# Sliding-window attention and a squared-ReLU FFN on one core: one planned order for all engines, over pairs of chunks

## The chip, the cores and the metric

The kernel runs on one core of one Trainium2 chip. The metric is the device time of one execution in microseconds (us). The engines are TensorE (PE, with its weight loads as PEld), VectorE (DVE), ScalarE (ACT), GpSimd (POOL) and SyncE (SP). Each engine takes its instructions in the order in which the program lists them. All DMAs here are issued from SP's queue.

## What is computed

Heads of 64 columns, a causal window of 64 keys, then a feed-forward layer over the heads put side by side:

```python
def _attn_ref(q, k, v):                    # (8, 8, 576, 64): batch, heads, tokens, columns
    scores = scale * np.matmul(q, k.transpose(0, 1, 3, 2))
    mask = (rel >= 0) & (rel < window)     # rel: query minus key; window = 64
    attn = softmax(np.where(mask, scores, -1e9))
    return np.matmul(attn, v)

def _moe_ref(x, w_in, w_out):              # x: (4608, 512), w_in: (512, 2048), w_out: (2048, 512)
    h = np.maximum(x @ w_in, 0.0)
    return h * h @ w_out
```

Inputs and output are float32; the kernel multiplies in fp16.

## The kernel before

The 4608 tokens (the batches one after the other) are 36 chunks of 128. A chunk's k, q and v are fetched as float32 (`fetch`, L100 to L110; one DMA of 256 KB each in runs of 256 bytes, two where a batch ends inside the chunk) and cast to fp16 by POOL (L200, L204, L208). POOL also moves the values by 64 partitions (`shift_v`, L212 and L214), since each block of 64 queries needs the 128 keys that end with it, and these must begin at partition 0. k and q are turned so that the head columns lie on partitions: the first 14 chunks by PE (`T`, L252) and copies out of PSUM (L267, L273), the others by a DMA transpose of 512 columns each (L276, L279). For the keys of the pair before, DVE copies 64 columns (`halo`, L240).

Attention of one chunk: scores (`S_`, L290, 16 matmuls of 64 columns), exp on ACT (L297), the mask as a minimum on DVE (L303), probabilities times values (`V`, L315), reciprocal and normalising on DVE (L322, L323). The result x is turned by PE (`X`, L334, first 16 chunks) or by a DMA transpose (`dma_xT`, L342).

The up-product (x times w_in) has two forms. For the first eight chunks `U` (L364) makes four blocks of 128 x 128 in one PSUM bank. For the groups of 512 tokens after that `UP` (L387) makes one block of 128 x 512 with four matmuls. ACT takes the ReLU out of PSUM (L371, L391); the square is ReLU times the PSUM value on DVE (L375, L395) or a Square on ACT (L381, L393); its place is the tile h2, of which there are two (512 tokens each).

The down-product of group 0 is plain (`O`, L431, 512 columns). From group 1 on it uses seven products of half size in place of eight (`out_seven`, L442): DVE forms sums of blocks of h2 (`hsum`, L456), PE multiplies them with prepared sums of w_out (`product`, L464, 256 columns), and ACT or DVE takes the banks out with the additions (`evac`, L478, L480). The sums of w_out are made once on DVE (`w_out_sum`, L412 to L418). w_in is scaled on DVE (L217), w_out cast on POOL (L222).

[...]

The order of work is set in two ways. Up to the first rounds it is the word list `FIRST`, which is issued word by word for all engines and for SP's queue: `fk0` fetches k of chunk 0, `fw0` a quarter of w_in, `T0` transposes, `U2.1` an up-product, `r` and `s` ReLU and square, `o` casts of w_out, `ws` its sums. It fetches chunks 0 to 3, then the four quarters of w_in (1 MB each), then the rest; w_out comes after chunk 7. From group 2 on, a loop gives each piece a fraction of the round and sorts by it:

```python
        ev = even(out_seven(g - 1))
        if g < NTB:
            ev += [(0.05 + 0.95 * t, s) for t, s in even([lambda f=f: UP(g, f) for f in range(FFC)])]
        if g + 1 < NTB:
            ev += attention(g + 1)
            ev += loads(4 * g + 6)
        for _, s in sorted(ev, key=lambda e: e[0]):
```

So in round g the down-product of group g-1 is interleaved with the up-product of group g, and between them stands the attention of group g+1, whose x goes to a DMA transpose at fractions 0.275 and 0.735 of the round.

Of the kernel before, what the change touches and what calls it, by code (L numbers as in the profile page):

```python
# [15 lines left out]
SQ_ACT = (0, 2, 4, 6, 8, 10, 12, 14)  # L16
FIRST = '''
fk0 fq0 fv0 fk1 fq1 kc0 fv1 qc0 T0 W4 fk2 vc0 ck0 cq0 vd0 fq2 S0 W6 ea0 fv2 kc1 eb0 ma0 qc1 fk3
mb0 vc1 T1 fq3 kc2 V0 W5 ck1 cq1 vd1 n0 fv3 S1 ea1 X0 fw0 qc2 eb1 ma1 x0 vc2 T2 mb1 vd2 ck2 cq2 V1
fw1 n1 S2 e2 kc3 fw2 X1 qc3 fw3 x1 fk4 m2 vc3 T3 fq4 vd3 ck3 cq3 V2 n2 S3 e3 X2 x2 m3 V3 n3 w0.0  # L20
X3 w0.1 x3 w0.2 w0.3 U0.0 U1.0 r0.0 fv4 w1.0 sa0.0 w1.1 U2.0 w1.2 r1.0 w1.3 U3.0 s1.0 r2.0 s2.0
U0.1 r3.0 w2.0 sa3.0 w2.1 U1.1 r0.1 w2.2 w2.3 U2.1 s0.1 r1.1 s1.1 U0.2 r2.1 fk5 w3.0 w3.1 U1.2
r0.2 w3.2 w3.3 sa0.2 U2.2 s2.1 fq5 kc4 r1.2 U0.3 s1.2 r2.2 fv5 qc4 s2.2 U1.3 r0.3 fk6 vc4 s0.3 T4
vd4 r1.3 fq6 U2.3 ck4 cq4 sa1.3 fv6 kc5 S4 r2.3 U3.1 qc5 fk7 e4 s2.3 vc5 T5 fq7 kc6 U3.2 r3.1 m4
cq5 vd5 ck5 V4 sa3.1 S5 n4 r3.2 fv7 U3.3 qc6 e5 fo0 vc6 X4 sa3.2 x4 T6 vd6 m5 r3.3 U4.0 fo1 ck6
cq6 s3.3 fo2 V5 kc7 r4.0 fo3 S6 n5 qc7 U4.1 e6 fk8 vc7 s4.0 fq8 X5 vd7 r4.1 U4.2 m6 x5 s4.1 V6
r4.2 T7 n6 U5.0 cq7 ck7 s4.2 X6 r5.0 o0 S7 x6 U4.3 e7 o1 s5.0 o2 U5.1 r4.3 m7 o3 s4.3 U5.2 r5.1
s5.1 V7 r5.2 fv8 o4 U6.0 n7 o5 s5.2 U5.3 o6 r6.0 o7 s6.0 X7 r5.3 U6.1 x7 o8 s5.3 U6.2 o9 r6.1
sa6.1 o10 ws0.0 U7.0 r6.2 ws1.0 o11 sa6.2 U6.3 ws0.1 r7.0 ws1.1 U7.1 r6.3 s7.0 fk9 o12 sa6.3 U7.2
o13 r7.1 fq9 kc8 ws0.2 U7.3 r7.2 s7.1 o14 fv9 sa7.2 O0.0 ws1.2 qc8 r7.3 fk10 ws2.0 vc8 T8 ws2.1  # L30
s7.3 O1.0 o15 fq10 cq8 ck8 vd8 O2.0 fv10 ws0.3 ws1.3 S8 ws2.2 kc9 O3.0 ws2.3 e8 qc9 fk11 vc9 O0.1
m8 fq11 vd9 T9 V8 ck9 cq9 fv11 O1.1 kc10 n8 fk12 qc10 S9 vc10 X8 e9 O2.1 fq12 x8 kc11 O3.1 vd10 m9
fv12 fk13 V9 qc11 T10 n9 O0.2 vc11 fq13 cq10 ck10 kc12 X9 S10 vd11 x9 O1.2 e10 fv13 T11 qc12 m10
fk14 O2.2 vc12 cq11 ck11 fq14 kc13 V10 S11 vd12 n10 fv14 O3.2 e11 X10 fk15 qc13 O0.3 m11 vc13 x10
fq15 V11 kc14 oe0 st0 T12 n11 vd13 fv15 O1.3 cq12 ck12 X11 qc14 oe1 st1 T13 x11 O2.3 vc14 ck13
cq13 vd14 O3.3 oe2 st2 oe3 st3 kc15 qc15 vc15 vd15
'''
# [3 lines left out]
def kernel(  # L41
# [15 lines left out]
    NCK = NT // P  # L57
    NB = S // 64
# [5 lines left out]
    NTB = NT // 512  # L64
    FQ = DFF // 4
    KH = FFC // 2
    NH = DM // 2
    NFIRST = 8

    const = ctx.enter_context(tc.tile_pool(name="const", bufs=1))  # L70
    stage = ctx.enter_context(tc.tile_pool(name="stage", bufs=17))
    st16 = ctx.enter_context(tc.tile_pool(name="st16", bufs=8))
    attw = ctx.enter_context(tc.tile_pool(name="attw", bufs=3))
    smallp = ctx.enter_context(tc.tile_pool(name="smallp", bufs=4))
    xtp = ctx.enter_context(tc.tile_pool(name="xtp", bufs=3))
    h2pool = ctx.enter_context(tc.tile_pool(name="h2pool", bufs=2))
    hrp = ctx.enter_context(tc.tile_pool(name="hrp", bufs=3))
    ps_up = ctx.enter_context(tc.tile_pool(name="ps_up", bufs=2, space=bass.MemoryType.PSUM))
    ps_out = ctx.enter_context(tc.tile_pool(name="ps_out", bufs=2, space=bass.MemoryType.PSUM))
    ps_att = ctx.enter_context(tc.tile_pool(name="ps_att", bufs=2, space=bass.MemoryType.PSUM))  # L80

    ctx.enter_context(tc.manual_schedule())


    put_off = []

    def later(n, fn):
        put_off.append([n, fn])

    def tick():  # L90
        for e in list(put_off):
            e[0] -= 1
            if e[0] <= 0:
                put_off.remove(e)
                e[1]()


    sts, k16s, q16s = {}, {}, {}

    def fetch(nm, i):  # L100
        src = {"k": k, "q": q, "v": v}[nm]
        b0, j0 = divmod(2 * i, NB)
        st = stage.tile([P, H, D], FP32, name=f"{nm}_st", tag="st")
        if j0 + 1 < NB:
            nc.sync.dma_start(
                out=st[:], in_=src[b0, :, 64 * j0:64 * j0 + P, :].rearrange("h p d -> p h d"))
        else:
            nc.sync.dma_start(
                out=st[0:64], in_=src[b0, :, 64 * j0:S, :].rearrange("h p d -> p h d"))
            nc.sync.dma_start(  # L110
                out=st[64:P], in_=src[b0 + 1, :, 0:64, :].rearrange("h p d -> p h d"))
        sts[nm, i] = st

    w_in_sb = const.tile([P, DMC, DFF], FP16, name="w_in_sb")
    w_out_sb = const.tile([P, FFC, DM], FP16, name="w_out_sb")
    wb_all = const.tile([P, 3, KH, NH], FP16, name="wb_all")
    hs_all = const.tile([P, 2, KH, 256], FP16, name="hs_all")
    early = h2pool.tile([P, FFC, 512], FP16, name="early", tag="h2")  # L120
    wb = [wb_all[:, i] for i in range(3)]

    def as_stage(ap, c=4):
        return ap.bitcast(FP32).rearrange("p (c n) -> p c n", c=c)


    tick_of = smallp.tile([P, 16], FP32, name="tick", tag="tick", bufs=1)
    nc.vector.memset(tick_of[:, 0:1], 0.0)
    nc.scalar.activation(out=tick_of[:, 1:2], in_=tick_of[:, 0:1], func=AF.Exp)

    def await_load(nm, i):

        nc.scalar.activation(out=tick_of[:, 1:2], in_=sts[nm, i][:, 0, 0:1], func=AF.Copy)

    wb_stage = as_stage(wb_all[:, 0:2].rearrange("p i k n -> p (i k n)"))
    hs_stage = as_stage(hs_all[:].rearrange("p i k n -> p (i k n)"))
    w_in_stage = [as_stage(early[:, 0:8].rearrange("p f t -> p (f t)")),
                  as_stage(early[:, 8:16].rearrange("p f t -> p (f t)")),
                  wb_stage, hs_stage]
    osb_all = const.tile([P, 3, 2, DM], FP32, name="osb_all")  # L140
    w_out_stage = [wb_stage, hs_stage, osb_all[:, 0:2].rearrange("p i m d -> p (i m) d"),
                   (as_stage(wb_all[:, 2].rearrange("p k n -> p (k n)"), 2), osb_all[:, 2])]

    def w_out_staged(f):
        at = w_out_stage[f // 4]
        return at[f % 4 // 2][:, f % 2] if f // 4 == 3 else at[:, f % 4]

    def fetch_w_in(quar):
        nc.sync.dma_start(
            out=w_in_stage[quar],  # L150
            in_=moe_w_in[:, quar * FQ:(quar + 1) * FQ].rearrange("(c p) n -> p c n", p=P))

    def fetch_w_out(quar):
        at = w_out_stage[quar]
        for n, part in enumerate(at if quar == 3 else (at,)):
            rows = 512 if quar < 3 else 256
            r0 = quar * 512 + n * rows
# [49 lines left out]
    def cast_v(i):  # L207
        nc.gpsimd.tensor_copy(out=v_evs[i % NV][:, :, 0:D], in_=sts["v", i][:])  # L208

# [429 lines left out]
```

## Time and profile before

| What | Value |
|---|---|
| Median of three timed runs | 314.78 us (313.43 to 315.09) |
| Span of the profiled execution, first to last instruction | 312.6 us |
| Mean TensorE clock granted in it | 0.973 of full speed |
| First up-product starts | 24.3 us |
| First round of seven products starts | 87.7 us |
| DMA: packets, bytes, share of 16 engines | 157,077; 55.05 MB; 75.8% on the main queue |

The page gives no other time of the profiled execution than its span. "Busy" counts the time in which an engine has an instruction under way; for PE that includes matmuls at a lower clock, so a busy PE isn't one at its best. The lines by stage have the busy time of each engine in a stretch of the span, with the granted clock (1.00 is full speed) and the DMA engines' share beside it. A line by instruction has minimum, median and maximum duration in ns.

### The profile page before, as it was taken

To read this page: it belongs to the slowest core of one execution; us is meant where nothing else is said; L and a number is where in the kernel's file an instruction comes from. 1 tells how busy PE (TensorE), PEld (TensorE's weight loads), DVE (VectorE), ACT (ScalarE), POOL (GpSimd) and SP (SyncE) were. 2 spreads that over 40 slices of the span, in tenths; PEclk is the share of its full clock that TensorE was granted. 3 is DMA by queue.
4 is the path that set the end of the run, shared out by engine and by line. 5 is a ranking of instruction groups with operands and counts; after the bars stand their busy time and mean duration, and the time that the engine had idled before them with its cause. 6 is when DMAs were issued, how large, how long until landed. Compare 5 with 4: busy or idle time off the path is not lost.

```text
span 312.6 us, 8069 instructions
## 1 busy us (share of the span) xinstructions
PE 289.9 (93%) x3263; PEld 201.3 (64%) x3263; DVE 215.4 (69%) x398; ACT 178.3 (57%) x282; POOL 134.6 (43%) x203
## 2 busy tenths in 40 slices
PE   3858899998998989999999999999996999999995
PEld 1448888965565656666666666666663666666684
DVE  4665959997676766875878486758766567546392
ACT  1333697762575647584766577576654575566500
POOL 4930888989833534371637353543254300000000
PEclk9955999999999999999999999999999899999999
DMA  7998999999669629899997799898799920400123
GB/s 181 230 363 243 228 271 388 210 219 221 151 186 211 132 66 242 178 153 138 274 171 166 185 238 166 169 221 203 151 154 210 220 59 19 151 2 0 69 102 102
DMA packets 157077, 55.05 MB, mean 176 GB/s; under 512 B 147824, under 2 KB 148848, under 8 KB 157040
## 3 DMA queue, kind: packets, MB, share of 16 engines
q1 hardware_dynamic: 157040, 54.54, 75.8%
q8 instruction: 25, 0.41, 0.6%
q14 instruction: 12, 0.10, 0.1%
HBM read 36.70 MB, written 9.44 MB: 148 GB/s over the span
## 4 chain that ended last, share of the span: by engine, by line
PE 77%; DVE 10%; ACT 7%; DMA 2%; issue 2%; SPq 0%; ACTq 0%
PE hps L387 30%; PE opsC L464 9%; PE opsD L464 8%; PE opsA L464 8%; PE hps L364 5%; PE opsB L464 4%; PE av L315 4%; PE sc L290 3%; PE ops L431 3%; ACT pm L297 2%; PE warm L403 2%; ACT hrelu L371 2%; DVE x_sb L323 2%; DVE pm L303 2%; DVE w_in_sb L217 1%
## 5 line engine op out<-in xcount | busy, mean ns | idle before, releaser
L387 PE MATMUL hps<-xT,w_in_sb 128*128 128x512 f16 x448 | 113.7, 382 | 3.0 <-DMA xT<-x_sb 2.7
L391 ACT ACTIVATE hrelu<-hps 128x512 f32<-128x512 f32 x112 | 66.8, 598 | 76.0 <-PE hps L387 75.9
L464 PEld LDWEIGHTS <-h 128*128 128x128 f16 x640 | 62.4, 98 | 23.0 <-issue 2.5
L387 PEld LDWEIGHTS <-w_in_sb 128*128 128x128 f16 x448 | 42.5, 98 | 36.2 <-DMA xT<-x_sb 2.9
L395 DVE SCALAR_TENSOR_TENSOR h<-hps,hrelu 128x512 f16<-128x512 f32 x56 | 38.6, 690 | 36.9 <-ACT hrelu L391 36.5
L200 POOL CAST k<-k_st 128x512 f16<-128x512 f32 x36 | 25.2, 701 | 79.6 <-DMA k_st<-in_k_dram 79.2
L297 ACT ACTIVATE pm<-sc 128x1024 f16<-128x1024 f32 (+1 forms) x38 | 35.6, 977 | 12.3 <-PE sc L290 12.3
L393 ACT ACTIVATE h<-hrelu 128x512 f16<-128x512 f32 x56 | 35.3, 630 | 1.8
L364 PE MATMUL hps<-xT,w_in_sb 128*128 128x128 f16 x512 | 33.6, 227 | 1.9 <-DVE h L375 1.3
L208 POOL CAST v_ev<-v_st 128x512 f16<-128x512 f32 x36 | 25.7, 713 | 18.8 <-DMA v_st<-in_v_dram 17.8
L364 PEld LDWEIGHTS <-w_in_sb 128*128 128x128 f16 x512 | 31.2, 102 | 2.9 <-issue 1.4
L464 PE MATMUL opsD<-wb_all,h 128*128 128x256 f16 x256 | 32.9, 273 | 0.0
L464 PE MATMUL opsA<-w_out_sb,h 128*128 128x256 f16 x240 | 31.9, 278 | 0.5
L464 PEld LDWEIGHTS <-hs_all 128*128 128x128 f16 x256 | 25.1, 98 | 8.9
L303 DVE TENSOR_TENSOR pm<-pm,mask_inner 128x1024 f16<-128x1024 f16 (+1 forms) x29 | 22.3, 769 | 9.5 <-ACT pm L297 9.4
L204 POOL CAST q<-q_st 128x512 f16<-128x512 f32 x35 | 24.0, 684 | 7.1 <-DMA q_st<-in_q_dram 6.5
L371 ACT ACTIVATE hrelu<-hps 128x512 f32<-128x512 f32 x32 | 18.8, 595 | 13.4 <-PE hps L364 12.1
L212 POOL COPY v_od<-v_ev 64x512 f16<-64x512 f16 x36 | 25.0, 696 | 2.3
L323 DVE TENSOR_TENSOR x_sb<-av,rden 128x512 f16<-128x512 f32 x36 | 24.9, 691 | 1.2
L214 POOL COPY v_od<-v_ev 64x512 f16<-64x512 f16 x35 | 24.9, 711 | 2.0
L480 DVE SCALAR_TENSOR_TENSOR osb_all<-opsD,u 128x512 f32<-128x512 f32 x16 | 11.0, 690 | 12.0 <-PE opsD L464 12.0
L375 DVE SCALAR_TENSOR_TENSOR h<-hps,hrelu 128x512 f16<-128x512 f32 x22 | 14.7, 681 | 6.3 <-ACT hrelu L371 6.2
(71 smaller groups left out, 331.1 us busy)
## 6 DMA issues: line engine op xcount, KB each, us to landing
k_st<-in_k_dram SPq DMA_DIRECT2D x32, 256.0 KB, 3.8
q_st<-in_q_dram SPq DMA_DIRECT2D x32, 256.0 KB, 4.2
v_st<-in_v_dram SPq DMA_DIRECT2D x32, 256.0 KB, 4.3
out_dram<-osb_all SPq DMA_DIRECT2D x14, 512.0 KB, 3.6
early<-in_moe_w_in_dram SPq DMA_DIRECT2D x2, 1024.0 KB, 8.8
out_dram<-osb_all SPq DMA_DIRECT2D x8, 256.0 KB, 2.2
wb_all<-in_moe_w_in_dram SPq DMA_DIRECT2D x1, 1024.0 KB, 11.4
hs_all<-in_moe_w_in_dram SPq DMA_DIRECT2D x1, 1024.0 KB, 15.4
```

Of the source, the lines that this page charges most:

```text
L200: nc.gpsimd.tensor_copy(out=k16s[i][:], in_=sts["k", i][:].rearrange("p h d -> p (h d)"))
L208: nc.gpsimd.tensor_copy(out=v_evs[i % NV][:, :, 0:D], in_=sts["v", i][:])
L297: nc.scalar.activation(out=pms[i][:, part], in_=scs[i][:, part], func=AF.Exp, scale=1.0 / float(D) ** 0.5)
L303: nc.vector.tensor_tensor(out=pms[i][:, part], in0=pms[i][:, part], in1=mask[:].rearrange("p (o a) r -> p o (a r)", o=1) .to_broadcast([P, ...
L323: nc.vector.tensor_tensor(out=xs[i][:], in0=avs[i][:, :, :, 0:D], in1=rden[:].to_broadcast([P, 2, 4, D]), op=ALU.mult)
L364: nc.tensor.matmul(hps[:, f, :], w_in_sb[:, c, (4 * fq + f) * P:(4 * fq + f + 1) * P], xT_of(g)[:, c, t0:t0 + P], start=(c == 0), stop=(c ...
L371: nc.scalar.activation(out=hr_of[i, fq][:], in_=hps_of[i, fq][:], func=AF.Relu)
L387: nc.tensor.matmul(hps[:], w_in_sb[:, c, f * P:(f + 1) * P], xT_of(g)[:, c, :], start=(c == 0), stop=(c == DMC - 1))
L391: nc.scalar.activation(out=hrelu[:], in_=hps[:], func=AF.Relu)
L393: nc.scalar.activation(out=h2_of(g)[:, f, :], in_=hrelu[:], func=AF.Square)
L395: nc.vector.scalar_tensor_tensor(out=h2_of(g)[:, f, :], in0=hps[:], scalar=0.0, in1=hrelu[:], op0=ALU.max, op1=ALU.mult)
L464: nc.tensor.matmul(banks[bank][:, m, :], a[:, kk, m * P:(m + 1) * P], w[:, kk], start=(first and kk == 0 and m == 0), stop=(kk == KH - 1), ...
```

## The change

Everything between setup and launch is written anew around a planner. Each operation is named and given a key (its priority), the engines that may run it with an assumed duration in us for each, the operations it comes after, and the buffers it uses. `Plan.order` then walks through time and issues operations one after the other; that sets the order on each engine and on SP.

```diff
+            for o in live:
+                t = opens(o)
...
+                ready = max(o["ready"], t)
...
+                w = min(((max(engines[r[0]], ready) + r[1], r[1], n)
+                         for n, r in enumerate(o["runs"])))
+                r = o["runs"][w[2]]
+                start = max(engines[r[0]], ready)
+                late = max(start - engines[r[0]], 0.0)
+                rank = (round(late, 1), o["key"])
```

`opens` gives the time at which the buffers are free. For each engine the operation with the shortest wait (in tenths of a us), and among these the lowest key, is next; where several engines may run it, the one that would be done first. A handoff to another engine counts 0.15 us, a DMA's landing 2.2 us after its end.

The buffers, all with fixed sizes:

```diff
+    plan.pool("wst", wb + hs)
+    plan.pool("st", tiles("st", NSTAGE, [P, 1024], FP32))
+    plan.pool("kq16", tiles("kq16", 4, [P, 1024], FP16))
+    plan.pool("kT", tiles("kT", 4, [P, HP, PT], FP16))
...
+    plan.pool("xT", tiles("xT", 5, [P, 2, DMC, P], FP16))
+    plan.pool("h2", tiles("h2", 4, [P, FFC, PT], FP16))
+    plan.pool("f2k", tiles("f2k", 12, [P, 512], FP32))
...
+    plan.pool("att", tiles("att", 2, [P, 2, 512], FP32, psum))
+    plan.pool("bk", tiles("bk", 4, [P, 512], FP32, psum))
```

`NSTAGE` is 6 (two pairs' k, q and v; before, 17 tiles of half the size). `h2` holds 256 tokens a tile. The four banks `bk` serve up-products, down-products and transposes alike; `att` serves scores and PV. `f2k` holds ReLU outputs, partial sums and output tiles.

The unit is a pair of chunks (256 tokens, 18 pairs). k and v are fetched in two DMAs a pair as before; q in one, two tokens to a partition, so a run is 512 bytes; the score block then has its columns in the order r, i, and is written to PSUM with a step of two:

```diff
+    def fetch_q(name, p):
...
+                in_=q[b, :, s:s + m, :].rearrange("h (p r) d -> p h (r d)", r=2))
...
+        scv = sc[:].rearrange("p a (h b i r) -> p a h b r i", h=HP, b=2, r=2)
...
+                    if n == 0:
+                        prev = at(f"kT.{p - 1}")[rs, hp, 192:256] if p else kT[rs, hp, 0:64]
+                        nc.tensor.matmul(scv[0:64, hh, hp, blk], prev, mv, start=True, stop=True)
+                        nc.tensor.matmul(scv[64:P, hh, hp, blk], kT[rs, hp, 0:64], mv,
+                                         start=True, stop=True)
```

The `halo` copy is gone: the first block of a pair reads the pair before. k, q and x of pairs 0 to 7 are turned by PE (eight transposes into one bank, one copy out by DVE or ACT), of pairs 8 to 17 by one DMA transpose of 1024 columns each. The order of the loads on SP is by keys (lowest first):

```diff
+    LOAD_KEYS = {0: -100, 1: -94, 2: -88, 3: -82, 4: -76, 5: -70}
+    WIN_KEYS = [-99, -98, -93, -92, -91, -90, -87, -86]
+    WOUT_KEYS = [-81, -80, -79, -78, -75, -74, -73, -72]
...
+        return LOAD_KEYS.get(p, p / 2 - 3.0)
```

So two eighths of w_in (512 KB each) come after pair 0, four after pair 1, two after pair 2; four eighths of w_out after pair 3, four after pair 4. Casts of k and q of pairs 0 to 3 and of the weights may run on POOL, DVE or ACT; the others, and all of v, on POOL. The value shifts go to DVE, for a whole pair at once:

```diff
+        V_.tensor_copy(out=vy[64:P, 2 * i:2 * i + 2].rearrange("p c h e -> p (c h e)"),
+                       in_=src[0:64].rearrange("p c h e -> p (c h e)"))
```

with a second copy for the other half, and a third where the ring of four pairs wraps.

The up-product is one operation for each two blocks of 128 hidden columns and 256 tokens (eight matmuls of 256 columns, half the bank each). The square is ReLU times ReLU out of SBUF, on DVE, ACT or POOL:

```diff
+            op(f"R.{p}.{j}", kx - 0.3, on([("ACT", 0.6)], lambda e, p=p, j=j: relu(p, j)),
+               after=[f"U.{p}.{j}"], uses=[f"u.{p}.{j}", f"hr.{p}.{j}"])
+            op(f"Q.{p}.{j}", kx, on([("DVE", 0.62), ("ACT", 0.64), ("POOL", 1.3)],
+                                    lambda e, p=p, j=j: square(e, p, j)),
```

All nine groups use the seven products (group 0 had the plain one), each in four operations of four matmuls (0.44 us assumed). All four output blocks of a group are stored by themselves (256 KB, runs of 1 KB). Keys put the attention of pair p at p/2 - 0.9, its up-products from p/2 to p/2 + 0.5 and the down-product of group g from g + 1 to g + 2, in rounds. A DMA transpose is assumed to take SP 1.3 us, a load of k or v 1.2, of q 1.8, of weights 1.45, a store 0.8.

Ahead of all stand 24 matmuls of 512 columns on zeros, in place of the 15 between the first chunks.

## The prediction

> **What bounds the kernel now.** I read the busy table first, then the chain of waits, then busy time by stage, then the clock in the first 34 us. The busy table:
>
> ```profile
> PE 289.9 (93%) x3263; PEld 201.3 (64%) x3263; DVE 215.4 (69%) x398; ACT 178.3 (57%) x282; POOL 134.6 (43%) x203
> ```
>
> TensorE (PE) is busy nearly throughout, and the chain that ended last gives it 77% of the span. Its busy time is not work at full speed, though. I sized the work by the chain in order of time: eight 256-column matmuls take 0.87 us (0.109 each), four of 512 columns 0.865 us (0.216), sixteen of 128 columns 0.89 us (0.056). From the timeline's starts, one chunk costs 0.31 us for scores, 0.32 for P times V, 0.46 for the k and q transposes, 0.22 for the x transposes.
>
> Work before: up, 448 x 0.216 + 512 x 0.056 = 96.9 + 28.6; down, 64 x 0.216 + 896 x 0.109 = 13.9 + 97.4; 36 chunks x (0.31 + 0.32) = 22.7; 14 x 0.46 + 16 x 0.22 = 9.9. Sum 269.4 us. The span is 312.6, so 43 us are lost. Where, the stages tell (columns: length, then busy time of PE, weight loads, DVE, ACT, POOL; clock; DMA share; GB/s):
>
> ```profile
> 0.80:24.30 23.50, 14.32 (x192) 8.89 (x192) 14.05 (x50) 7.50 (x11) 12.77 (x24) 0.83 0.99 271
> 24.30:58.90 34.60, 31.94 (x578) 30.01 (x577) 26.87 (x55) 23.15 (x39) 23.80 (x38) 0.92 0.98 273
> 58.90:88.40 29.50, 28.45 (x381) 19.01 (x378) 24.28 (x49) 16.63 (x26) 24.38 (x36) 1.00 0.84 196
> ...
> 120.60:149.20 28.60, 28.50 (x281) 18.61 (x280) 21.61 (x35) 18.66 (x30) 13.41 (x18) 1.00 0.94 171
> ...
> 208.00:242.20 34.20, 31.45 (x321) 20.39 (x318) 25.36 (x41) 21.11 (x33) 15.12 (x23) 0.99 0.87 184
> ```
>
> To 88.4 us the work done is 28.6 + 13.9 + 12 chunks x 0.63 + 6.4 + 12 x 0.22 = 59.1 us: **29.3 us lost at the start**. From 88.4 to 296.3 (seven rounds of one down-group with the next up-group) it is 96.9 + 7 x 12.2 + 24 x 0.63 + 0.9 = 198.3 of 207.9: 9.6 lost, most of it in the rounds at 88 (32.2 long) and 208 (34.2, with a 2.65 us wait for one transposed x and a clock of 0.50 after it). The other rounds run at 28.6 to 29.7. The tail, 296.3 to 308.7, is 12.2 us of pure work, and 3.9 us go to the last eviction and store.
>
> At the start the DMA share is 0.99 and 0.98: transfers bound it. The order is four chunks of k, q, v, then all of w_in (4 MB), so the first up-product starts at 24.3 us. The clock adds to it:
>
> ```profile
> 14.00:16.00 2.00, 1.00 (x24) 0.80 (x23) 1.97 (x6) 0.55 (x1) 1.89 (x4) 1.00 1.11 212
> 16.00:18.00 2.00, 1.39 (x25) 1.17 (x25) 1.08 (x3) 1.07 (x2) 1.88 (x4) 0.63 0.96 321
> 22.00:24.00 2.00, 0.78 (x18) 0.64 (x19) 1.19 (x4) 0.00 (x0) 0.00 (x0) 0.50 1.05 386
> 28.00:30.00 2.00, 2.00 (x21) 2.00 (x20) 0.39 (x1) 1.13 (x2) 0.00 (x0) 0.50 0.70 143
> 30.00:32.00 2.00, 2.00 (x38) 2.00 (x36) 1.15 (x3) 1.12 (x2) 0.61 (x1) 0.96 0.52 115
> ```
>
> The reader is to see that sparse matmuls leave a clock of 0.50, and that 5 to 6 us of dense ones pass before it is whole again.
>
> **PE work after.** Up: all 1152 matmuls of 256 columns, x 0.109 = 125.3 (before 125.5: the 128-column ones were dearer per column). Down: 9 groups x 112 x 0.109 = 109.7 (before 111.3). Scores: the first block of each pair splits its matmuls in two, 8 more per pair at 0.31/16, 18 x 0.155 = 2.8 more. k and q transposes for 16 chunks instead of 14: 0.9 more. Sum 271.4 us, **2.0 more**. Each 256-column matmul now loads its own weights (98 ns beside 109 in the L464 rows), hidden there, so hidden here.
>
> **The start.** Rates from the windows: 256-byte rows of k and v at 237 GB/s, weights at 391. A pair is 1.05 MB of k and v, 4.4 us, and 0.52 MB of q in 512-byte runs. No row shows such runs; between the two rates they take 1.3 to 2.2 us, and I take 1.8, the middle. So 6.2 us a pair and 1.33 a weight eighth, from 0.8 us, plus 2 us to land (k: issued 0.81, cast at 3.97, 1.1 of it transfer). In SP's new order pair 0 lands at 9.0, the first quarter of w_in at 11.7, pair 1 at 17.9, quarters 2 and 3 at 23.2, pair 2 at 29.4, the last quarter at 32.1, pair 3 at 38.3, half of w_out at 43.6, pair 4 at 49.8, the rest of w_out at 55.1. From landing to transposed x a pair takes cast 0.8, transposes 0.5, copy 0.8, scores 0.3, two exps 2.04, mask 0.79, PV 0.3, normalising 0.9, x transposes 0.45, copy 0.8: 7.7 with handoffs about 8. So up-products start at 17 instead of 24.3, at half clock, and can go on with pairs 1, 2, 3 at 26, 37.5 and 46.5. Between them PE idles for want of data. It is dense from about 57: then w_out is cast, and down-group 0 must run anyway, because the four h2 buffers are held by pairs 0 to 3 and up-product 4 waits for one (nothing later on PE but down-group 1 and attention can pass it, and these fill the gap).
>
> Done by 57: 32 up-products x 0.87 = 27.8, four pairs of attention and transposes x 2.8 = 11.2, a first quarter of down-group 0 1.7, transposes 0.9: 41.6. Lost 15.4. DVE is at 24.3 of 29.5 us in the stage at 59 already and takes over the value shifts, so I add 4.6 for queues that don't hand on at once: 20 lost. Bounds: 13 with none of that, 29.3 if everything gained is given back. **Gain 9, between 0 and 16.**
>
> **Other engines.** POOL loses 71 shifts of 0.70 (50 us). DVE gains two or three 64-partition shifts a pair; nearest rows are f16 copies of 512 at 0.22 to 0.29 and of 256 at 0.32, so 0.3 to 0.8 each for 1056, take 0.5: 20 us; six more sums, 5; three more evictions, 2; it loses the halo copies, 5.4. Some of its 78 squares go to POOL. At most 240 us of 300: not the bound, if the durations hold. [...] The square was one PSUM and one SBUF operand; now both are SBUF. Row for two SBUF operands:
>
> ```profile
> L456 DVE TENSOR_TENSOR hs_all<-h x16: 678/684/1098, 87.7 to 299.1; 128x1024 f16<-128x1024 f16 x16
> ```
>
> With POOL idle at the end such sums take 0.68; the same under POOL casts up to 1.10. By this row 70 squares cost DVE 0 to 29 us more (0.42 each); I take 0.1 each, nearer the median, 7 us, and none of it on the path. [...]
>
> A square on POOL is not in the trace; its casts of 512 take 0.61 to 0.71, two operands between once and twice that; POOL falls to some 85 us plus 20 to 60 such squares, so nothing on the path.
>
> **SP's queue.** Its rows:
>
> ```profile
> L276 SPq DMA_TRANSPOSE kT<-k x22: 1205/1452/2888, 88.9 to 247.0; - x22
> L105 SPq DMA_DIRECT2D k_st<-in_k_dram x32: 444/577/2167, 0.8 to 240.2; - x32
> ```
>
> Half as many transposes, twice as wide. An issue of 1024 columns is not shown: 1.2 us if per instruction, 2.4 if per column; I take 2.4, as bytes double. A round then asks of SP 6 x 2.4 + 10 x 0.7 + 4 x 0.4 = 23 us of 28.6, where before it was 12 x 1.2 + 12 x 0.7 + 0.9 = 24. The planner counts 1.3, so its order issues them later than the chip wants. Cover is that attention is ordered 0.9 round (26 us) ahead of its up-products, where the late x of the round at 208 was ordered 0.3 round ahead.
>
> **The rounds and the end.** The wait at 236.8 and its slow clock (about 5 us) go. I expect new ones: PE waits in order behind planned times with 0.15 us for a handoff, and U, O and early transposes share four banks. I take 7 lost for 9.6, bounds 3 and 25 (the upper end is 3 a round, as in the worst rounds now). End 3.9, unchanged: one 256 KB store as before.
>
> Sum: 271.4 + 20 + 7 + 3.9 = 302.3 us of span, 10.3 less than the profiled 312.6. The page gives no time for that execution beside its span; the median of the runs, 314.78, lies 2.2 above it. **Forecast 304.5 us.**
>
> **Rivals.**
> - Better: start at its bound 13 and rounds at 3, sum 291.3, time 293.5. For it: rounds that lose 0.1 exist (120.6). Against: no slack anywhere in the start. Chance 0.12.
> - The gain doesn't come: start stays at 29.3 and rounds at 9.6, because the first 60 us are bound by all engines and the DMA together (DVE 24.3 of 29.5). Sum 314.2, time 316.4; with half of it 311. Chance 0.14.
> - Slower, SP falls behind: each wide transpose takes 1.1 us more than the plan counts, 6.6 a round; stores queue behind a transpose that waits for its x, output buffers stay held, the ReLU waits for a buffer and PE for a PSUM bank. It decides from the point where SP's 23 us plus waits at its head pass the round's 28.6, so 5.6 of waits. If 6.6 reach PE in 5 rounds: 304.5 + 33 = 337; half of it, 321. I take 321. Against: before carried the same 24 us. Chance 0.21.
> - Forecast case, 298 to 312: chance 0.53.
>
> Faster by over 0.5% (below 313.2; about what a measurement of this kernel can tell from no change): 0.53 + 0.12 + a little of the second = 0.67; within: 0.09; slower: 0.24. The range reaches from the better rival to just short of the slower one's milder price: 294 to 319.
>
> **What would show it.** Right: first up-product near 17 us, PE dense from 55 to 60, rounds of 28.5 to 29.5 without waits on transposed x, 271 us of work in about 302. [...]

## The result, and the profile after

The changed kernel takes 326.23 us (median of four runs, 325.65 to 326.7); the kernel before, beside it, 314.93 (313.43 to 316.0). The ratio is 1.036, 95% interval 1.031 to 1.041: slower, where 304.5 was forecast, and outside the forecast's range. Now and then an execution of a kernel takes over 1.5% longer than its fastest (the kernel before took 311.72 to 318.89 us in 25 executions); the ratios below leave these out, the medians don't.

The page of the changed kernel begins so (the span, the busy table, TensorE's row in 40 slices, the chain of waits):

```profile
span 323.9 us, 8613 instructions
PE 311.2 (96%) x3672; PEld 257.1 (79%) x3672; DVE 230.0 (71%) x367; ACT 190.9 (59%) x287; POOL 86.0 (27%) x78
PE   8698999989999999999999999999999999999995
PE 84%; DMA 6%; DVE 6%; ACT 1%; POOL 1%; issue 1%; SPq 0%; DVEq 0%; POOLq 0%; ACTq 0%
```

TensorE is busier than before (96% for 93%) and has 84% of the chain for 77%. No engine took the bound from it: it has more to do. VectorE's 230 is within the 240 that the prediction allowed. POOL's 86 is less than it said: 85 were forecast without squares, and the 86 hold 19 squares (23.1 us). The stages (columns as before: length, PE, weight loads, DVE, ACT, POOL; clock; DMA share; GB/s):

```profile
126.90:158.90 32.00, 32.00 (x386) 26.82 (x385) 22.99 (x37) 20.79 (x33) 10.37 (x9) 1.00 1.04 212
158.90:191.00 32.10, 32.02 (x386) 26.80 (x385) 22.96 (x35) 20.24 (x32) 9.03 (x9) 1.00 1.04 216
191.00:223.00 32.00, 32.00 (x386) 26.86 (x385) 21.99 (x38) 20.29 (x32) 6.84 (x6) 1.00 0.78 146
307.70:323.90 16.20, 12.22 (x112) 10.71 (x110) 7.35 (x11) 2.42 (x4) 0.00 (x0) 1.00 0.24 81
```

These rounds contain no wait of TensorE at a whole clock, and yet last 32.0 us, where the better rounds of before took 28.6 to 29.7. A round that is longer without a wait has dearer work in it. The timeline of TensorE in one of them shows which (start, duration, line, shape, count). First the kernel before, the scores of two chunks:

```profile
236.77 0.64 PE L290 MATMUL sc<-qT,kT 64*128 64x64 f16 x32
237.34 0.39 PE L464 MATMUL opsA<-w_out_sb,h 128*128 128x256 f16 x2
```

And the changed kernel, the scores of one pair:

```profile
204.55 0.24 PE L316 MATMUL att<-qT,kT 64*64 64x64 f16 x1
204.55 0.24 PE L317 MATMUL att<-qT,kT 64*64 64x64 f16 x1
204.56 0.24 PE L316 MATMUL att<-qT,kT 64*64 64x64 f16 x1
204.56 0.24 PE L317 MATMUL att<-qT,kT 64*64 64x64 f16 x1
204.73 0.23 PE L320 MATMUL att<-qT,kT 64*128 64x64 f16 x2
204.89 0.24 PE L316 MATMUL att<-qT,kT 64*64 64x64 f16 x1
...
205.76 0.68 PE L320 MATMUL att<-qT,kT 64*128 64x64 f16 x18
206.37 0.39 PE L577 MATMUL bk<-wb,h 128*128 128x256 f16 x2
```

From start to start: before, 32 matmuls in 0.57 us, 18 ns each. After, the last 18 take 0.61 us (205.76 to 206.37), 34 ns each; and a group of four halves and two wholes, of which the first chunk has four, takes 0.34 us (204.55 to 204.89). (The wholes of the fourth group run on into the 16 of the second chunk, hence 18.) Together 1.82 us a pair (204.55 to 206.37). Eighteen pairs: 32.8 us, where the prediction had 14.0 (22.7 for all attention less P times V, and 2.8 for the split). TensorE's work is 271.4 + 18.8 = 290.2 us.

Two causes were possible for these scores: the write to PSUM with a step of two, or the alternation of tile shapes (64 x 64 for the halves, 64 x 128 for the wholes). A third was that reading q is to blame. Theory A in the expectations is that write and alternation both act, A1 that the write does. The first nine experiments tell these apart.

### The profile page after: what moved, and what is told of

It is laid out like the page before. It is cut to its first block, busy times and chain, and to the rows that moved or that the text cites. A ratio compares the mean times of both kernels' runs of the same rounds, so it can differ in the third digit from the quotient of the medians.

```text
span 323.9 us, 8613 instructions
## 1 busy us (share of the span) xinstructions
PE 311.2 (96%) x3672; PEld 257.1 (79%) x3672; DVE 230.0 (71%) x367; ACT 190.9 (59%) x287; POOL 86.0 (27%) x78
## 4 chain that ended last, share of the span: by engine, by line
PE 84%; DMA 6%; DVE 6%; ACT 1%; POOL 1%; issue 1%; SPq 0%; DVEq 0%; POOLq 0%; ACTq 0%
PE bk L520 34%; PE bk L577 33%; DMA st<-in_k_dram 6%; PE att L320 5%; PE att L343 3%; PE att L316 3%; PE bk L661 3%; DVE wb L501 2%; PE bk L296 2%; DVE pm L329 1%; PE bk L302 1%; POOL kq L275 1%; DVE x L368 1%; DVE w_out_sb L501 0%; DVE qT L275 0%
## 5 line engine op out<-in xcount | busy, mean ns | idle before, releaser
L520 PE MATMUL bk<-xT,w_in_sb 128*128 128x256 f16 x1152 | 148.4, 274 | 1.7 <-ACT xT L273 0.7
L524 ACT ACTIVATE f2k<-bk 128x512 f32<-128x512 f32 x144 | 85.2, 598 | 82.8 <-PE bk L520 81.4
L520 PEld LDWEIGHTS <-w_in_sb 128*128 128x128 f16 x1152 | 110.9, 98 | 16.4 <-issue 1.2
L532 DVE TENSOR_TENSOR h<-f2k 128x512 f16<-128x512 f32 x56 | 39.9, 714 | 35.1 <-ACT f2k L524 35.0
L577 PE MATMUL bk<-w_out_sb,h 128*128 128x256 f16 x432 | 57.7, 273 | 0.0
L275 POOL CAST kq<-st 128x1024 f16<-128x1024 f32 x29 | 34.2, 1178 | 63.1 <-DMA st<-in_k_dram 31.0
L530 ACT ACTIVATE h<-f2k 128x512 f16<-128x512 f32 x69 | 43.3, 630 | 2.0
L324 ACT ACTIVATE pm<-att 128x1024 f16<-128x1024 f32 x36 | 35.5, 1020 | 13.8 <-PE att L320 13.8
L587 DVE SCALAR_TENSOR_TENSOR f2k<-bk,f2k 128x512 f32<-128x512 f32 x45 | 31.0, 688 | 16.3 <-PE bk L577 16.1
L577 PE MATMUL bk<-wb,h 128*128 128x256 f16 x288 | 38.6, 273 | 0.0
L532 POOL TENSOR_TENSOR h<-f2k 128x512 f16<-128x512 f32 x19 | 23.1, 1223 | 55.3 <-issue 31.0
L343 PEld LDWEIGHTS <-pm 128*64 128x64 f16 x576 | 12.4, 112 | 9.6 <-issue 5.7
L577 PE MATMUL bk<-wb,hs 128*128 128x256 f16 x144 | 18.8, 273 | 0.9 <-DVE wb L501 0.9
```

Source lines behind the costliest of these rows:

```text
L275: (V_ if eng == "DVE" else G_).tensor_copy(out=o, in_=i)
L324: A_.activation(out=at(f"pm.{p}.{c}")[:], in_=at(f"sc.{p}.{c}")[:], func=AF.Exp, scale=1.0 / float(D) ** 0.5)
L343: nc.tensor.matmul(av[64 * blk:64 * blk + 64, h // 4, h % 4, 0:65], pm[:, h % 2, h0:h0 + 64], vv[:, c, h, 0:65], start=True, stop=True)
L520: nc.tensor.matmul(ps[:, f], w_in_sb[:, c, f0:f0 + P], xT[:, :, c, :], start=(c == 0), stop=(c == DMC - 1))
L524: A_.activation(out=at(f"hr.{p}.{j}")[:], in_=at(f"u.{p}.{j}")[:], func=AF.Relu)
L530: A_.activation(out=o, in_=hr, func=AF.Square)
```

## Experiments on the scores

All ratios are against the kernel before, run beside them on the same chip.

**The halves grouped.** All halves of a chunk first, then its wholes:

```diff
-        for hp in range(HP):
-            for blk in range(2):
+        for blk in range(2):
+            for hp in range(HP):
```

> The kernel after, with the sixteen split score matmuls (64x64 tiles) of a pair's first block put one after the other ahead of the eight whole ones (64x128), instead of alternating four and two. Nothing else moves. In the trace after, a pair's scores take 1.82 us on PE (before 0.62), and the first chunk's take 0.343 for each four-and-two. [...] Theory B (it is the number of matmuls, 24 for 16, and their longer duration, whatever their order): no change, 326. Theory C (the scores are not the cause; the planned order is): no change, 326.

318.25 us, ratio 1.016 (1.010 to 1.022). The pair's scores fall from 1.82 to 1.13 us:

```profile
200.49 0.24 PE L316 MATMUL att<-qT,kT 64*64 64x64 f16 x1
...
200.84 0.84 PE L320 MATMUL att<-qT,kT 64*128 64x64 f16 x24
201.62 0.50 PE L577 MATMUL bk<-wb,h 128*128 128x256 f16 x3
```

The 16 halves now need 0.35 us instead of four times 0.18; the wholes still cost 33 ns each. Alternation was 0.69 us a pair, 12.4 us over 18 pairs, and gave 8 of time.

**Written in order, read alternately.**

```diff
-        scv = sc[:].rearrange("p a (h b i r) -> p a h b r i", h=HP, b=2, r=2)
+        scv = sc[:].rearrange("p a (h b i r) -> p a h b i r", h=HP, b=2, r=2)
...
-                    mv = qT[rs, :, hp, 32 * n:32 * n + 32]
+                    mv = qT[rs, :, hp, 32 * n:32 * n + 32].rearrange("p r i -> p i r")
```

> The kernel after, with the scores written to PSUM in steps of one, and q's columns read in the permuted order instead (64 single columns, alternately from two places 1 KB apart). Same values in the same places. Theory A1 (the step of two on the write side is what doubles a score matmul): the eight whole matmuls of a second chunk go from 34 to 18 ns each; a pair's scores fall by 0.3 to 0.55 us, the time by 6 to 10 us, to 316 to 320. Theory A2 (reading q in two pieces is what slows it): no gain, or slower, since the reads are now more scattered, 326 or above. Theory C: no change.

327.32 us, ratio 1.042 (1.035 to 1.050): no gain.

```profile
210.32 0.73 PE L320 MATMUL att<-qT,kT 64*128 64x64 f16 x18
210.99 1.05 PE L577 MATMUL bk<-wb,h 128*128 128x256 f16 x8
```

From start to start the 18 wholes take 0.67 us, 37 ns each. This run could not clear or convict the write: it exchanged it for a read that takes single columns from two places in turn, and that is a little dearer still.

**Both of these edits.**

> Both edits at once: split matmuls together, and scores written in steps of one. Theory A: a pair's scores fall from 1.82 to about 0.75 us (24 x 0.018, plus 16 x 0.018, plus two changes of shape), 18 x 1.07 = 19 us: 307, faster than the kernel before. Theory B: at most what the step alone gives. Theory C (planned order): 326.

319.75 us, ratio 1.020 (1.014 to 1.027): the grouping's gain alone, again, and not the 307 of theory A.

**q fetched like k**, in runs of 256 bytes, so that read and write are both in order; the halves still alternate.

```diff
-        for p0, n, b, s, m in pieces(PT * p, PT, 2):
-            nc.sync.dma_start(
-                out=st[p0:p0 + n],
-                in_=q[b, :, s:s + m, :].rearrange("h (p r) d -> p h (r d)", r=2))
+        for c in range(2):
+            fetch_kv(q, name, p, c)
...
-                    mv = qT[rs, :, hp, 32 * n:32 * n + 32]
+                    mv = qT[rs, hp, 64 * n:64 * n + 64]
```

> The kernel after, with q fetched as k is (two DMAs of 256 KB a pair, runs of 256 bytes), so that q's columns are read and scores written in order; the split of the first block stays as it is. Theory A (write step, or read in two pieces): a pair's scores fall as in the run with steps of one, 6 to 10 us; against it stands what the 512-byte runs had saved: at most 0.9 us for each of the first four pairs at the start (6.6 us instead of 5.7 to 6.2 a pair), so 318 to 322 in all. Theory C: slower than after by up to 4 us, 326 to 330.

322.96 us, ratio 1.030 (1.024 to 1.037). The alternating part now repeats every 0.29 us, and the last 18 wholes take 0.37 us from start to start, 21 ns each where the changed kernel had 34:

```profile
204.35 0.44 PE L317 MATMUL att<-qT,kT 64*128 64x64 f16 x18
204.72 1.05 PE L574 MATMUL bk<-wb,h 128*128 128x256 f16 x8
```

So with neither step the wholes are cheap again and the alternation remains.

**Grouped, and the scores written in the order of reading** (r, i); the exponential puts the tokens back in order as it writes fp16:

```diff
-        scv = sc[:].rearrange("p a (h b i r) -> p a h b r i", h=HP, b=2, r=2)
+        scv = sc[:].rearrange("p a (h b r i) -> p a h b r i", h=HP, b=2, r=2)
...
-        A_.activation(out=at(f"pm.{p}.{c}")[:], in_=at(f"sc.{p}.{c}")[:], func=AF.Exp,
+            out=at(f"pm.{p}.{c}")[:].rearrange("p a (g i r) -> p (a g) r i", i=32, r=2),
+            in_=at(f"sc.{p}.{c}")[:].rearrange("p a (g r i) -> p (a g) r i", i=32, r=2),
```

> The split matmuls grouped, as before; and the scores written to PSUM in the order in which q's columns are read (two runs of 32, each written in steps of one). The exp puts them in token order instead: it reads PSUM in order and writes its fp16 result with a step of two. So both sides of a score matmul are in order, with q still fetched in 512-byte runs. So far: grouping alone 318.3 us, grouping with q read column by column alternately 319.8, so that either a step on the write side or a scattered read costs the same 16 ns. Theory A1 (the step on the write side is the cost in the kernel after, reading two runs of 32 is free): a pair's scores go from 1.13 to 0.7 us, 18 x 0.43 = 8 us: 310. Theory A2 (reading in two runs costs as well): 318. Theory D (the exp pays for it: its write with a step of two takes longer than 1.02 us): ACT is busy 60%, so up to 0.5 us each would stay hidden; above that slower than 318.

314.61 us, ratio 0.999 (0.994 to 1.003). The scores of a pair take 0.70 us (123.66 to 124.36), less than the 0.775 forecast:

```profile
123.66 0.21 PE L316 MATMUL att<-qT,kT 64*64 64x64 f16 x1
...
123.91 0.52 PE L320 MATMUL att<-qT,kT 64*128 64x64 f16 x24
124.36 0.50 PE L579 MATMUL bk<-w_out_sb,h 128*128 128x256 f16 x3
```

The whole slowdown is gone, though the 310 of theory A1 was not reached. The stepped write has moved to ScalarE, where it isn't free: 1.31 us for an exponential of 1.02.

**q fetched like k, and grouped.**

> q fetched in 256-byte runs (323.0 us by itself) and the split matmuls grouped. Theory A: the two costs add up, a pair's scores take some 0.7 us instead of 1.5, 18 x 0.5 = 8 to 9 us: 314 to 315, the time of the kernel before. Against the run with the exp's permutation (310 by theory A1) the difference is what 512-byte runs save at the start, up to 4 us. If it is 310 as well, the runs save nothing.

317.13 us, ratio 1.008 (1.005 to 1.011). The scores are as cheap here; against the run before it, fetching q in one DMA of 512-byte runs is worth some 2.5 us.

**The kernel before with a step of two in its score writes.** The probe from the other side:

```diff
-        scv = sc[:].rearrange("p a (h b t) -> p a h b t", h=HP, b=2)
+        scv = sc[:].rearrange("p a (h b i r) -> p a h b r i", h=HP, b=2, r=2)
```

> The kernel before, with one change: each score matmul writes its 64 columns to PSUM with a step of two, in two passes. The queries inside a block of 64 then stand in another order than the mask assumes, so the probabilities are not the reference's; every instruction is there, with the same sizes. Theory A1 (write step): 576 matmuls x 16 ns = 9 us on PE, which is the bound in the rounds: 313.4 + 24 x 0.27 to 36 x 0.27 = 320 to 323. Theory A2 (reading in two pieces): no change, 313.

319.79 us, ratio 1.013 (1.005 to 1.021), and 32 matmuls take 1.00 us from start to start where they took 0.57:

```profile
125.60 1.07 PE L290 MATMUL sc<-qT,kT 64*128 64x64 f16 x32
126.60 0.39 PE L465 MATMUL opsA<-w_out_sb,h 128*128 128x256 f16 x2
```

**The kernel before with its first block split**, in alternation, without a step:

```diff
+                    if i % 2 == 0 and blk == 0:
+                        for u in range(2):
+                            nc.tensor.matmul(
+                                scv[64 * u:64 * u + 64, hh, hp, blk, :],
+                                kT[r0:r0 + 64, hp, k0 + 64 * u:k0 + 64 * u + 64], mv,
```

> The kernel before, with the first block's score matmul of every even chunk split in two of 64x64, in the alternating order of the kernel after (four small, two whole). Values are unchanged. Theory A (a change of tile shape costs some 0.1 to 0.16 us): the even chunk's scores go from 0.31 to about 1.0 us, 18 x 0.65 = 12 us; those of the rounds, 12 of 18, are on the path, those at the start partly: 321 to 325. Theory B (only the number of matmuls): 144 more x 18 ns = 2.6 us, 316.

325.61 us, ratio 1.036 (1.026 to 1.046). Four halves and two wholes repeat every 0.29 us:

```profile
126.62 0.22 PE L293 MATMUL sc<-qT,kT 64*64 64x64 f16 x4
126.78 0.20 PE L298 MATMUL sc<-qT,kT 64*128 64x64 f16 x2
126.91 0.22 PE L293 MATMUL sc<-qT,kT 64*64 64x64 f16 x4
```

At the 18 ns of one shape, six would take 6 x 18 ns = 0.11. Each of the two effects, put alone into the kernel before, is there: both are shown.

**The exponential reads with a step and writes in order**, the rest as in the permuted one:

```diff
-            out=at(f"pm.{p}.{c}")[:].rearrange("p a (g i r) -> p (a g) r i", i=32, r=2),
-            in_=at(f"sc.{p}.{c}")[:].rearrange("p a (g r i) -> p (a g) r i", i=32, r=2),
+            out=at(f"pm.{p}.{c}")[:].rearrange("p a (g i r) -> p (a g) i r", i=32, r=2),
+            in_=at(f"sc.{p}.{c}")[:].rearrange("p a (g r i) -> p (a g) i r", i=32, r=2),
```

> As the run with the exp's permutation (314.6 us; its exp took 1.31 us where an exp in order takes 1.02, so 36 x 0.29 = 10 us more on ACT), but the exp reads PSUM with a step of 32 and writes in order. The order of all engines is the same. If the write with a step was what lengthened it, the exp falls to 1.02 us and the time by up to 3 us (ACT is 63% busy, but in the stage from 30 to 70 us it is above 85%); if a read with a step costs as much, no change.

314.27 us, ratio 1.000 (0.996 to 1.004). The exponential is back at 1.02:

```profile
L324 ACT ACTIVATE pm<-att x36: 1006/1018/1047, 10.7 to 260.2; 128x1024 f16<-128x1024 f32 x36
```

ScalarE got 36 x 0.29 = 10 us back and the time did not move: ScalarE isn't on the path. This is the mended kernel in what follows.

## Experiments on the start

With the scores mended the kernel is level with the one before, not 10 us faster. I counted the matmuls of each trace in time, each at the prediction's price (a pair's scores at 0.62 whatever they took), in us of work done (the last three rows belong to runs that come below):

```
by            50 us    70     100     140
before         24.9   44.1    70.3   108.5
changed        26.5   42.9    67.5   104.2
mended         26.8   42.1    66.5   105.1
no sums        26.8   43.4    71.4   109.7
half of w_out  26.2   42.0    66.9   105.3
both cuts      26.8   41.1    67.0   105.5
```

By 50 us the new order leads by 1.9 us; by 100 it is 3.8 behind. Most of that is lost from 50 to 70 us (15.3 us of work for 19.2). What fills 50 to 100? In the mended kernel's trace VectorE is busy 8.4 of 10 us from 50 to 60, 9.6 from 60 to 70 and 9.7 to 9.9 after that, with transfers at a share of about 1.0 (the windows from 70 us on, columns as above):

```profile
70.00:80.00 10.00, 8.15 (x117) 7.06 (x115) 9.92 (x14) 6.57 (x10) 6.07 (x6) 1.00 1.06 201
80.00:90.00 10.00, 9.48 (x115) 8.03 (x114) 9.66 (x17) 4.38 (x7) 4.64 (x5) 1.00 0.97 232
90.00:100.00 10.00, 8.45 (x137) 7.02 (x136) 9.91 (x14) 7.25 (x11) 4.58 (x4) 1.00 1.00 214
```

TensorE's longest waits there, from 40 to 105 us, are these (us in total, times, longest):

```profile
PE bk L579 <- DVE wb L503: 1.6, 2, 1.1
PE bk L579 <- DVE w_out_sb L275: 1.4, 1, 1.4
PE bk L296 <- POOL kq L275: 1.4, 2, 0.8
PE att L345 <- DVE pm L331: 1.3, 3, 0.5
```

So VectorE and the transfers (for which POOL's casts wait) are the two candidates. Three runs move single parts of the change back, on the kernel with the permuted exponential.

**Value shifts on POOL** instead of VectorE:

```diff
-        V_.tensor_copy(out=vy[64:P, 2 * i:2 * i + 2].rearrange("p c h e -> p (c h e)"),
+        G_.tensor_copy(out=vy[64:P, 2 * i:2 * i + 2].rearrange("p c h e -> p (c h e)"),
...
-        op(f"sv.{p}", K + 0.1, on([("DVE", 0.8)], lambda e, p=p: shift_v(p)),
+        op(f"sv.{p}", K + 0.1, on([("POOL", 2.2)], lambda e, p=p: shift_v(p)),
```

> The run with the exp's permutation, with the value shifts given back to POOL (2.2 us a pair assumed). The other order of operations follows from it. What is still open: with the score matmuls repaired the kernel is only level with the one before, where 10 us less were forecast; from 45 to 100 us DVE is busy 9.8 of every 10 us, and its two-operand instructions take up to 1.52 us for 0.69 while POOL works. Theory E (DVE, lengthened by POOL, is the bound of the start): without some 12 us of shifts there the start gets shorter by 3 to 6 us, 309 to 312. Theory F (the transfers bound the start): no change, 314; or slower, as POOL's casts come later.

316.28 us, ratio 1.005 (1.001 to 1.009): not the gain of theory E. VectorE looks the better place, by 1.7 us with intervals that overlap: a shift of 1056 takes 1.27 to 1.33 us on POOL in the mean of its two lines, and 0.43 on VectorE by the median.

**No squares on POOL:**

```diff
-            op(f"Q.{p}.{j}", kx, on([("DVE", 0.62), ("ACT", 0.64), ("POOL", 1.3)],
+            op(f"Q.{p}.{j}", kx, on([("DVE", 0.62), ("ACT", 0.64)],
```

> The run with the exp's permutation, with no squares on POOL (19 of 144 there, most of them before 85 us, each 1.0 to 1.5 us with two operands from SBUF); DVE and ACT take them. [...]

314.15 us, ratio 0.998 (0.995 to 1.002): nothing either way. In its trace (an execution of 317.24 us) VectorE is busy 8.1 of 10 us from 40 to 100, for 9.8 with the permuted exponential alone: less load there, and no gain.

**w_in after pairs 0 and 1**, not between them:

```diff
-    WIN_KEYS = [-99, -98, -93, -92, -91, -90, -87, -86]
+    WIN_KEYS = [-93.8, -93.4, -93, -92, -91, -90, -89.6, -89.2]
```

> The run with the exp's permutation, with all of w_in fetched after pairs 0 and 1, as in the kernel before, instead of between the first pairs. Forecast's view (the transfers bound the start): up-products begin 4 to 6 us later, time up by 3 to 5 us, 318 to 320. Theory E (DVE bounds the stage from 45 to 100 us): what is lost before 35 us is mostly caught up, at most 1.5 us, 314 to 316.

318.18 us, ratio 1.013 (1.009 to 1.017). The early w_in is worth 3.6 us; this part of the forecast's start holds, and what is lost before 35 us isn't caught up, against theory E.

The next six take the mended kernel. The first three keep its order on every engine.

**Without the eight sums of w_out** (VectorE):

```diff
-               tt(e, *w_sum(kind, h))), after=o_of + prev,
+               ws_none(kind, h)), after=o_of + prev,
```

> After_expread with the same order on every engine, but the eight sums of w_out's blocks aren't made: the products that read a sum read the unsummed block of w_out in its place, so the output is another one. In the profile of the kernel with the permuted exponential these eight took VectorE from 64.35 to 74.2 us, about 9.9 us of a VectorE that is never idle from 44 to 62 us and from 64 to 102. Theory D1 (VectorE sets the pace of the start): 4 to 10 us shorter than after_expread's 314.27, so 304 to 310. Theory D2 (the transfers set it): 0 to 1.5 us shorter, VectorE gets idle time and TensorE waits for x or for q and k instead.

311.95 us, ratio 0.994 (0.990 to 0.998), beside 1.000 (0.996 to 1.004) for the mended kernel: 2.3 us less by the medians, between what D2 allowed (1.5) and what D1 asked for (4), with intervals that overlap. The profiled execution, with a span of 307.8, is the fastest of the ten. The sums of the windows from 60 to 100 us, first the mended kernel, then this one:

```profile
sum 40.00, PE 35.59 PEld 29.70 DVE 39.08 ACT 25.68 POOL 22.23; mean PE 8.90 PEld 7.42 DVE 9.77 ACT 6.42 POOL 5.56
```

```profile
sum 40.00, PE 39.31 PEld 33.86 DVE 31.83 ACT 28.49 POOL 19.49; mean PE 9.83 PEld 8.46 DVE 7.96 ACT 7.12 POOL 4.87
```

With 7.2 us less on VectorE, TensorE's idle time falls from 4.4 to 0.7 us. All of the 4.4 ended on VectorE, 2.0 of it on these sums themselves, which the products read. In the mended kernel's trace the chain that ended last runs through them from 65.7 to 74.8 us. So this run takes away both some load of VectorE and a wait for these eight instructions; it doesn't tell the two apart.

**Half of w_out's columns fetched:**

```diff
-            out=wst(f"wo.{i}").rearrange("p (f n) -> p f n", f=2),
-            in_=moe_w_out[256 * i:256 * i + 256, :].rearrange("(f p) n -> p f n", p=P))),
+            out=wst(f"wo.{i}").rearrange("p (f n) -> p f n", f=2)[:, :, 0:256],
+            in_=moe_w_out[256 * i:256 * i + 256, 0:256].rearrange("(f p) n -> p f n", p=P))),
```

> After_expread with the same order on every engine, but only the first 256 of 512 columns of w_out are fetched, the other half of each staging tile keeps what was there, so the output is another one. That is 2.1 MB fewer; at the 193 to 277 GB/s that the profile of the permuted exponential shows from 40 to 90 us it is 7.6 to 10.9 us of transfers. Theory D1 (VectorE sets the pace of the start): 0 to 1.5 us shorter than 314.27. Theory D2 (transfers): 4 to 9 us shorter, 305 to 310, with the waits of POOL for k, q and v mostly gone from 40 to 100 us.

314.65 us, ratio 1.000 (0.995 to 1.005). The share falls (below) without the 4 us or more of D2; VectorE stays full and the time stays:

```profile
60.00:70.00 10.00, 9.43 (x142) 7.63 (x140) 9.94 (x14) 7.49 (x12) 7.01 (x6) 1.00 0.86 184
70.00:80.00 10.00, 8.54 (x121) 7.34 (x120) 9.92 (x15) 6.96 (x10) 5.22 (x5) 1.00 0.90 183
```

**Both cuts:**

> Both cuts at once: no sums of w_out's blocks and half of w_out's columns fetched, same order as after_expread; the output is another one. D1: as with the sums alone left out, within 1.5 us. D2: as with the half of w_out alone left out, within 1.5 us. If each stands behind the other, the two single cuts give little and this one 4 us or more beyond the better of them.

313.16 us, ratio 0.997 (0.993 to 1.001), within 1.5 us of the sums alone, as VectorE's theory asks, though its interval reaches 1. Its trace (the slowest of the ten) has no more work done by 100 us than the mended kernel's, 67.0 us for 66.5, though VectorE is busy 8.2 of 10 us from 40 to 100 for 9.5.

What this shows is limited. From 60 to 100 us TensorE's waits end on VectorE, and fewer bytes of w_out shorten nothing. But VectorE's load as a whole isn't shown to set the pace: two traces with less of it, this one and the one without POOL's squares, are no better. And the transfers aren't cleared before 60 us: in the mended kernel's trace the chain that ended last goes through a fetch of q from 50.1 to 57.7. Of some 10 us between the mended kernel and the forecast the runs account for 2.3 at most; the rest is open.

Three tries then relieve VectorE with the whole computation kept; each lets the plan make its order anew.

**Casts open to ScalarE, no squares on POOL:**

```diff
-        ch = [("POOL", 1.3)] + ([("DVE", 1.1), ("ACT", 1.1)] if early else [])
+        ch = [("POOL", 1.3)] + ([("DVE", 1.1), ("ACT", 1.1)] if early else [("ACT", 1.1)])
...
-        op(f"cv.{p}", K, on([("POOL", 1.3)], lambda e, p=p: copy(
+        op(f"cv.{p}", K, on([("POOL", 1.3), ("ACT", 1.1)], lambda e, p=p: copy(
```

> After_expread with the squares of POOL given to VectorE and ScalarE and the casts of q, k and v open to ScalarE too (1.1 us in the plan against POOL's 1.3): POOL's operations fall from about 80 to about 40, the plan makes its order anew. A try at a faster kernel: if VectorE is late because POOL holds it up (two-operand operations of 0.68 us take up to 1.52), the stretched operations go from most to few and it ends 2 to 5 us sooner, 309 to 312; if the transfers set the pace it stays at 313.5 to 315; if ScalarE gets too full, 316 or more.

319.49 us, ratio 1.017 (1.008 to 1.027).

**Casts of w_out not on VectorE:**

```diff
-on([("POOL", 1.3), ("DVE", 1.0), ("ACT", 1.1)],
+on([("POOL", 1.3), ("ACT", 1.1)],
```

> After_expread with the casts of w_out open to POOL and ScalarE only; VectorE's four (1.53, two in 2.13 and 0.69 us from 47.5 to 62.2 us in the profile of the permuted exponential) go, 4.3 us, and the plan makes its order anew. A try at a version faster than both kernels. If VectorE sets the pace from 60 to 100 us, as the run without the eight sums shows (9.9 us off VectorE, ratio to the kernel before 0.9941 against 0.9999), 4.3 us off it are worth some 1 to 2 us: 312.5 to 313.5. If the new order loses as much: 314 to 315.

318.81 us, ratio 1.016 (1.009 to 1.022).

**Copies of turned k, q and x on ScalarE from pairs 2 and 3 on:**

```diff
-                op(f"{s}T.{p}", ak, on([("DVE", 0.8), ("ACT", 1.0)], lambda e, p=p, s=s: copy(
+                op(f"{s}T.{p}", ak, on(([("DVE", 0.8)] if p < 3 else []) + [("ACT", 1.0)], lambda e, p=p, s=s: copy(
```

> After_expread with the copies of the turned k and q of pairs 3 to 7 and of x from pair 2 to 7 out of PSUM on ScalarE only (1.02 us there, 0.68 on VectorE): up to five copies, 3.4 us, leave VectorE between 44 and 100 us for a ScalarE that is busy 6.7 of 10 us there. Same reasoning: 1 to 2 us shorter than after_expread, 312.5 to 313.5; where ScalarE's queue makes the relus late instead, 315 or more.

317.05 us, ratio 1.010 (1.006 to 1.013).

None is faster; they are 2.8 to 5.2 us slower than the mended kernel. In their traces TensorE waits for other things: ReLUs and evictions that end late on ScalarE and VectorE (with the casts, 3.9 and 2.7 us from 40 to 105), the mask again (with w_out's casts, 6.2), a cast on POOL (with the copies, 2.4). No version with the whole computation is clearly faster than the kernel before. Whether another order with the same load could be is open.

## Why the prediction was wrong, by its own steps

- **The step that failed: "Scores: the first block of each pair splits its matmuls in two, 8 more per pair at 0.31/16, 18 x 0.155 = 2.8 more."** It counted instructions at the price of a row whose matmuls all have one shape and write in order. The eight extra ones weren't the cost: with the scores mended a pair takes 0.70 us for the 0.62 priced before, 1.4 more in all. The change of shape was 0.69 us a pair and the stepped write 0.43: 12.4 and 7.7 us more, 21.5 with the 1.4, in place of 2.8. Put the missing 18.8 us into the forecast's sum and it gives 321.1 for a span of 323.9.
- **The diff's stepped write was costed at nothing**, and the prediction named no cover for it. No row of the trace had one, so it should have been bounded from both sides like the other unknowns.
- No rival had dearer matmuls. The change of shape had no price in the sum, and the runs give it: four halves and two wholes in alternation repeat every 0.29 us (the kernel before with its first block split, and q fetched like k), where six at the 18 ns of one shape take 0.11. What TensorE does in the rest of that time is in no trace.
- **Start, 20 lost (13 to 29.3): the second term that was mis-sized.** In the changed kernel it comes out near: 323.9 - 290.2 of work - 4.0 at the end - 6.4 in the rounds leaves 23.3. That was luck: the dear scores filled time in which TensorE would have waited. With the scores mended, work 270.0 and span 313.0, the same subtraction leaves 32.6, above the bound of 29.3, and the up-products of pair 6 start no sooner (121.7 us for 121.8). In the changed kernel the first up-product came at 18.9 us (17 forecast), and the transposed x of pairs 1 to 3 was ready at 30.7, 44.8 and 58.1 (26, 37.5 and 46.5). "4.6 for queues that don't hand on at once" was the whole allowance for all that. How the loss divides between VectorE, the transfers and the order is open (above).
- **"DVE is at 24.3 of 29.5 us in the stage at 59 already and takes over the value shifts"** saw it. The step after it, "at most 240 us of 300: not the bound", judged by the mean over the span. The mean was right (230), but in the stage from 40 to 100 us VectorE was busy 9.3 of 10 us, and 9.5 with the scores mended.
- **"By this row 70 squares cost DVE 0 to 29 us more (0.42 each); I take 0.1 each".** The 0.42 as worst case was too small: operations with two SBUF operands take 0.68 us by the median and such a sum up to 1.53 beside POOL, 0.85 more (rows below); in the traces of both kernels those that run while POOL is idle take at most 0.69. The 7 us in all were more than enough: in the changed kernel the 56 squares on VectorE took 39.9 us, 1.9 more than at their shortest (0.679 each), and POOL was busy for only 27% of the span. And without POOL's squares nothing was gained.
- **Rounds, 7 lost; end, 3.9.** A round's work is 13.95 up, 12.21 down and 2 x (1.82 + 0.64) attention, 31.1 of 32.0: 0.9 a round, 6.4 in seven; the end 4.0. Both right, and the wait for a late x is gone. With the scores mended a round takes 29.75 us.
- **SP falls behind** (the slower rival) didn't happen. The forecast's sign was missed by another mechanism. A wide transpose took 1.6 to 1.7 us by the median, nearer to the price per instruction (1.2) than to the 2.4 taken:

```profile
L425 SPq DMA_TRANSPOSE kT<-kq x10: 1237/1616/2547, 94.0 to 221.9; - x10
L457 SPq DMA_TRANSPOSE xT<-x x10: 1232/1722/3228, 143.6 to 276.3; - x10
```

Rows of VectorE's sums in the kernel with the permuted exponential (minimum, median, maximum):

```profile
L503 DVE TENSOR_TENSOR wb<-w_out_sb x2: 1405/1462/1519, 64.4 to 67.1; 128x1024 f16<-128x1024 f16 x2
L503 DVE TENSOR_TENSOR h<-h,h x18: 679/683/1525, 59.4 to 299.5; 128x1024 f16<-128x1024 f16 x18
```

## What to carry to other kernels

Price an instruction by its access pattern and by its neighbour in the queue, not by its count: a stepped destination nearly doubled these small matmuls (31 to 34 ns for 18), a change of tile shape more than doubled them (0.29 us for four and two, for 0.11), and no busy share shows it; compare starts, not durations. Where a layout must be permuted, look for the operand for which the permutation is free: here the exponential's read of PSUM (1.02 us with the step as without). An engine at 71% of the span can be nearly full in one stage (here VectorE, 9.3 of 10 us from 40 to 100), so test a cover stage by stage; whether that engine's load or single waits for it set the pace takes a run of its own. And a gain at the start can be lost again soon after: here a lead of 1.9 us at 50 us was a lag of 3.8 at 100.

## What the runs showed of the hardware

- A 64-column score matmul takes 18 ns of TensorE's queue with an ordered write to PSUM (32 in 0.57 us) and 31 to 34 with a step of two (32 in 1.00 us, 18 in 0.61); reading single columns from two places in turn, written in order, 37 (18 in 0.67 us).
- Alternating 64 x 64 and 64 x 128 tiles (four and two) takes 0.29 us, 0.34 with the stepped write, where six matmuls at the 18 ns of one shape take 0.11.
- ScalarE's exponential of 1024 columns takes 1.02 us in order and with a stepped read of PSUM, and 1.31 with a stepped fp16 write.
- VectorE operations of 0.68 us with two SBUF operands take at most 0.69 while POOL is idle and up to 1.55 beside it (a mask at 177.3 us of the changed kernel); a copy of 0.43 (value shift) up to 1.32.
